# Rows of 34 chunks turned on VectorE and moved by SP transfers, in an attention and mixture-of-experts kernel

## The chip, the cores and the metric

The kernel runs on one core of one Trainium2 chip. The metric is the device time of one execution in microseconds (us); times are medians of several runs. The engines are PE (TensorE, matrix products; PEld is its loading of weights), DVE (VectorE), ACT (ScalarE), POOL (GpSimd) and SP (SyncE, which here only issues DMA transfers). SBUF is the working memory with 128 partitions, PSUM the memory into which PE writes.

## The reference

Attention over channels gives x, 20224 rows of 256 numbers; a gate gives each row to one of eight experts, 2528 rows to each, and each expert applies two matrices.

```python
qn = q / (np.linalg.norm(q, axis=1, keepdims=True) + 1e-06)
kn = k / (np.linalg.norm(k, axis=1, keepdims=True) + 1e-06)
s = kn.transpose(0, 2, 1) @ qn / tau
a = softmax(s)                       # over the last axis
x = (v @ a).reshape(B * S, D)        # 20224 x 256

logits = x @ w_gate
# pairs (row, expert) in descending order of logit: a row goes to the first
# expert that still has room, at most N // E = 2528 rows to each
for e in range(E):
    mask = assigned == e
    h = np.maximum(x[mask] @ w1[e], 0.0)
    out[mask] = h @ w2[e]
```

## The kernel before

The kernel has three parts. First the scores, the softmax and the gates' logits are worked out. Then x is made and stored in DRAM (x_d). Then the eight experts follow (p = 0 to 7), and beside them the routing (which rows belong to the next experts) goes on in `route` and `compact`, mostly on DVE, with short products on PE.

An expert's 2528 rows are 20 tiles of 128 (the last has 96), and the tiles are cut into chunks: (2, 4, 4, 4, 4, 2) for expert 0 and (4, 4, 4, 4, 4) for the others, 41 chunks in all. A chunk (p, c) goes through these steps:

- `load_x` (L999) queues one indirect DMA per tile on POOL, which gathers the rows into xg (three buffers); `gather` (L1008) issues the next one of the queue at fixed places of the order.
- `turn` (L1020) brings 128 of the 256 columns (kb 0 or 1) of all rows of a chunk to partitions: PE transposes tile by tile into pt in PSUM, ACT writes xH (the rounded high part), and DVE writes xL (what is left). After kb 1 it calls `load_x` for the chunk three further on, whose xg this one frees.
- `layer1` (L1048) has eight blocks (fb 0 to 7) of six products each into ph (three buffers); ACT makes hH = relu(ph), and DVE hL, the remainder.
- `layer2` (L1083) has 24 products per tile into py (two buffers); ACT copies py to y (six buffers), and POOL scatters y to out by an indirect DMA.

The chunks are taken in a staggered manner: layer 1 of chunk c, then layer 2 of chunk c - 1, with the two turns of chunk c + 1 before tiles 0 and 3 of that layer 2. The head of the next expert (p + 1, 0) is turned in the last layer 2 of expert p, between its tiles, and (p + 1, 1) in the blocks 2 and 7 of its own expert's first layer 1.

Every engine works through its instructions in the order in which the program emits them. That order is written out by hand: `Order` (L841) keeps estimated clocks for PE (`o.pe`) and DVE (`o.dve`). `o.post(ready, cost, fn, unit)` puts a DVE step into a first-in first-out list, from which it is emitted when the estimated clock of DVE reaches it; `o.flush(unit)` emits all up to a unit; steps of the routing fill the gaps between. `want(key, fn)` runs fn as soon as a result of the routing stands in the order.

SP has loads to issue only up to the attention part; while the experts run it issues none.

Of the kernel before, what the change touches and what calls it, by code (L numbers as in the profile page):

```python
# [8 lines left out]
F32 = mybir.dt.float32  # L9
# [6 lines left out]
OP = mybir.AluOpType  # L16
# [58 lines left out]
EARLY_PRIO = 4  # L75
COMPACT_PRIO = 2
SLACK = 450
DEPTH = 3


@with_exitstack
def attention_moe(ctx: ExitStack, tc: tile.TileContext, q, k, vt, tau, wg, w1t, w2t, tabs, out):
# [865 lines left out]
    def cols_of(p, c):  # L948
        a = sum(cuts[p][:c])
        return range(a, a + cuts[p][c])  # L950

    def n_in(col):
        return 128 if col < NCOL - 1 else LASTC
# [45 lines left out]
    def load_x(p, c):  # L999
        idx = routed[p]["src"]  # L1000
        xg = ffx.tile([128, 4, C], F32, name="xg", bufs=3)
        for i, col in enumerate(cols_of(p, c)):
            queue.append(lambda i=i, col=col, n=n_in(col): P.indirect_dma_start(  # L1003
                out=xg[:n, i, :], out_offset=None, in_=x_d,
                in_offset=bass.IndirectOffsetOnAxis(ap=idx[:n, col:col + 1], axis=0)))
        xgs[p, c] = xg

    def gather(behind=None):  # L1008
# [7 lines left out]
    phs = []  # L1016
    turned = [0]
    lows = {}

    def turn(p, c, kb):  # L1020
        xg = xgs[p, c]
        nt = n_of(p, c)
        if kb == 0:
            xH = ffx.tile([128, 2, 512], F32R, name="xH")
            xL = ffx.tile([128, 2, 512], F32R, name="xL")
            xts[p, c] = (xH, xL)
        xH, xL = xts[p, c]
        o.flush(turned[0])
        pt = ps_t.tile([128, 512], F32, name="pt")
        for i, col in enumerate(cols_of(p, c)):  # L1030
            n = n_in(col)
            PE.transpose(pt[:, i * 128:i * 128 + n].bitcast(F32R), xg[:n, i, kb * 128:(kb + 1) * 128].bitcast(F32R),  # L1032
                         identr[:n, :n])
        S.activation(xH[:, kb, 0:nt], pt[:, 0:nt], AF.Copy)  # L1034

        def low():
            V.tensor_tensor(xL[:, kb, 0:nt], pt[:, 0:nt], xH[:, kb, 0:nt].bitcast(F32), op=OP.subtract)  # L1037
        o.pe += 220
        o.hook()
        unit[0] += 1  # L1040
        turned[0] = unit[0]
        o.post(o.pe + TURN_LAT, 605, low, unit[0])
        ahead = chunks.index((p, c)) + 3
        if kb == 1 and ahead < len(chunks):
            p_, c_ = chunks[ahead]
            want(("idx", p_), lambda: load_x(p_, c_))

    def layer1(p, c, inserts):  # L1048
        o.flush(turned[0])
# [33 lines left out]
    def layer2(p, c, h, inserts):  # L1083
        hH, hL = h
        o.flush(lows[p, c])
        wH, wL = wt[p, 1]
        o.until(("out", p))
        idx = routed[p]["idx"]
        for i, col in enumerate(cols_of(p, c)):
            for fn in inserts.get(i, ()):  # L1090
                fn()
            n = n_in(col)
            tk = slice(i * 128, i * 128 + n)
            py = ps_2.tile([128, 512], F32, name="py")
            j = 0
            for fb in range(8):
                d = slice(fb * C, (fb + 1) * C)
                for l, w in ((hH, wH), (hH, wL), (hL, wH)):
                    PE.matmul(py[:n, 0:C], lhsT=l[:, fb, tk], rhs=w[:, d], start=(j == 0), stop=(j == 23))  # L1099
                    j += 1  # L1100
                    if j % 2 == 0:
                        o.tick(2 * 109)
            y = ffx.tile([128, C], F32, name="y", bufs=6)
            S.activation(y[:n], py[:n, 0:C], AF.Copy)  # L1104
            P.memset(spacer[:, 0:1], 0.0)  # L1105
            sd = P.indirect_dma_start(out=out, out_offset=bass.IndirectOffsetOnAxis(ap=idx[:n, col:col + 1], axis=0),  # L1106
                                      in_=y[:n], in_offset=None)
            for s_ in scat:
                tc.declare_no_dep(sd.ins, s_.ins, reason="each token is written once")
            scat.append(sd)  # L1110
            settle()
            gather()

    with tc.manual_schedule():
        o.dve = FIRST_LAT
        plan()
        cut_w = [None]

        def first_w():
            load_w(0)  # L1120
            cut_w[0] = [o.pe + LOAD_LAT] + list(SPLIT)

        want(("ei", 0), first_w)
        for i, (b, c) in enumerate(TODO):
            xs = vp.tile([128, T, GW], F32, name="xs", bufs=2)
            for t in range(0, T, 2):
                x_tiles(b, c, t, xs, C, o.tick)
                settle()
                if cut_w[0] and o.pe > cut_w[0][0] and len(cut_w[0]) > 1:
                    split_piece(0, *cut_w[0].pop(1))  # L1130
                if i + 1 == len(TODO) and t > 0:
                    store_x(b, c, xs, {2: 0, 4: 4, 6: 6}[t], t + 2)
            if i + 1 < len(TODO):
                store_x(b, c, xs)
        o.until(("ei", 0))
        settle()
        o.until(("idx", 0))
        actx.close()
        cctx.close()
        ffx = ctx.enter_context(tc.tile_pool(name="ffx", bufs=2))  # L1140
        ffx.tile([128, PAD_X], F32, name="pad_x", bufs=1)
        ps_1 = ctx.enter_context(tc.tile_pool(name="ps_1", bufs=3, space=PSUM))
        ps_2 = ctx.enter_context(tc.tile_pool(name="ps_2", bufs=2, space=PSUM))
        ps_t = ctx.enter_context(tc.tile_pool(name="ps_t", bufs=1, space=PSUM))
        o.margin = MARGIN
        for c in range(2):
            load_x(0, c)
            while queue:
                gather()
        load_x(0, 2)  # L1150
        for i, q_, eng in cut_w[0][1:]:
            split_piece(0, i, q_, eng)
        idle = ps_1.tile([128, 512], F32, name="ph")
        for i in range(START_TICKS):
            o.tick(200)
            PE.matmul(idle, lhsT=wt[0, 0][0][:, 0:128], rhs=wt[0, 0][0][:, 512:1024], start=(i == 0),
                      stop=(i == START_TICKS - 1))
        turn(0, 0, 0)
        turn(0, 0, 1)
        for p in range(E):  # L1160
            last = p == E - 1
            def turn_at(c, kb):
                return lambda: turn(p, c, kb)

            turns = [] if last else [0, 1]

            def next_turn(force=False):
                if not turns:
                    return
                if force:  # L1170
                    o.until(("idx", p + 1))
                    settle()
                    while queue:
                        gather()
                    while o.pe < routed[p + 1]["time"] + GATHER_LAT:
                        o.tick(100)
                if done.get(("idx", p + 1)) and o.pe >= routed[p + 1]["time"] + GATHER_LAT:
                    turn(p + 1, 0, turns.pop(0))

            if not last:  # L1180
                want(("ei", p + 1), lambda p=p: load_w(p + 1))
            nchunk = len(cuts[p])
            h = {}
            pieces = {} if p == 0 else {at: [lambda q_=q_: split_piece(p, 1, q_, None)] for q_, at in enumerate((1, 3, 4, 6))}
            h[0] = layer1(p, 0, {**pieces} if p == 0 else {2: [turn_at(1, 0)], 7: [turn_at(1, 1)], **pieces})
            for c in range(1, nchunk):
                if p == 0 and c == 1:
                    turn(p, 1, 0)
                    turn(p, 1, 1)
                    layer2(p, 0, h[0], {})  # L1190
                    h[1] = layer1(p, 1, {4: [turn_at(2, 0)], 7: [turn_at(2, 1)]})
                    continue
                h[c] = layer1(p, c, {})
                ins = {}
                if c + 1 < nchunk:
                    for at, kb in ((0, 0), (3, 1)):
                        ins.setdefault(min(at, cuts[p][c - 1] - 1), []).append(turn_at(c + 1, kb))
                elif not last:
                    def w1(p=p):
                        o.until(("ei", p + 1))  # L1200
                        settle()
                        g = split_w(p + 1, 0, V)
                        for _ in g:
                            o.dve += 600
                    ins = {min(1, cuts[p][c - 1] - 1): [w1]}
                layer2(p, c - 1, h[c - 1], ins)
            layer2(p, nchunk - 1, h[nchunk - 1], {i: [next_turn] for i in range(1, 4)})
            while turns:
                next_turn(True)

# [62 lines left out]
```

## Time and profile before

| | us |
|---|---|
| median of three runs | 1333.44 (1333.43 to 1334.2) |
| profiled execution | 1331.89 |
| its span, first to last instruction | 1330.1 |
| transposes of gathered rows on PE | 320, median 231 ns each, from 346 to 1290 us of the span |
| DMA engines, mean busy share while experts run | 0.18 to 0.20 |

The profile counts an engine as busy while an instruction runs on it; products on PE are pipelined, so two may overlap, and the pitch from one to the next says more than the duration of one. Rows of a timeline give start, duration, engine, line, operation, what is written and read, its form, and in brackets the idle time in front of it and what ended that.

### The profile page before, as it was taken

The page shows a single profiled execution, that of the slowest core. Times are in us where ns is not written, and L with a number is a line of the kernel's source. Part 1 is how long each engine was busy: PE and PEld are TensorE (multiplying, and loading weights), DVE is VectorE, ACT ScalarE, POOL GpSimd, SP SyncE. Part 2 cuts the span into 40 slices and gives each one's busy share as a digit, 9 for nine tenths or more (in the row PEclk, how much of TensorE's full clock was granted, in tenths as well). Part 3 has the DMA queues.
Part 4 walks back from the last instruction along what each step waited for, and adds up shares of the span by engine and source line. Part 5 has one row for each costly group of instructions (what it writes and reads, how often), then busy time and mean ns, then how long its engine had stood idle before and what let it go on. Part 6 is the DMA issues. An engine that isn't in the chain of part 4 may idle for free.

```text
span 1330.1 us, 23080 instructions
## 1 busy us (share of the span) xinstructions
PE 1301.9 (98%) x9162; PEld 1157.0 (87%) x9162; DVE 761.9 (57%) x1912; ACT 528.3 (40%) x1189; POOL 386.9 (29%) x642
## 2 busy tenths in 40 slices
PE   7989999999899999999999999999999999999998
PEld 6877877888788888998999898988998998999998
DVE  6765395768478568658757757673443224333321
ACT  5554452235234234425324524345543234334331
POOL 0000010000352443254333333343344334434222
PEclk9999999999999999999999999999999999999999
DMA  8999884235312112023111211131122113111000
GB/s 287 381 360 355 273 273 176 96 127 191 100 55 92 52 48 99 29 64 107 40 41 49 102 41 45 41 105 45 45 74 83 42 47 109 48 45 51 28 29 32
DMA packets 53707, 143.14 MB, mean 108 GB/s; under 512 B 7776, under 2 KB 28640, under 8 KB 48992
## 3 DMA queue, kind: packets, MB, share of 16 engines
q1 hardware_dynamic: 14544, 62.40, 13.4%
q0 software_dynamic: 17664, 58.22, 13.3%
q10 hardware_dynamic: 21392, 21.06, 4.6%
q8 instruction: 72, 1.18, 0.4%
q14 instruction: 35, 0.29, 0.1%
HBM read 99.97 MB, written 41.68 MB: 106 GB/s over the span
## 4 chain that ended last, share of the span: by engine, by line
PE 55%; issue 5%; POOL 2%; DVE 1%; ACT 0%; POOLq 0%
PE ph L1067 26%; PE py L1099 25%; PE pc L508 2%; PE pt L1032 1%; POOL out_dram L1106 1%; PE pi L717 1%; PE pc L521 0%; POOL spacer L1105 0%; DVE m L464 0%; DVE f L489 0%; DVE xL L1037 0%; POOLq L1268 0%; ACT hH L1070 0%; DVE eq L486 0%; DVE L L683 0%
## 5 line engine op out<-in xcount | busy, mean ns | idle before, releaser
L1099 PE MATMUL py<-ua,hH 128*128 128x256 f32 (+1 forms) x2560 | 469.4, 283 | 0.0
L1067 PE MATMUL ph<-xH,ua 128*128 128x512 f32 (+3 forms) x1312 | 412.5, 388 | 3.3 <-issue 1.9
L1099 PEld LDWEIGHTS py<-ua,hH 128*128 128x128 f32 (+1 forms) x2560 | 391.7, 187 | 0.4
L1099 PE MATMUL py<-ua,hL 128*128 128x256 f32 (+1 forms) x1280 | 360.4, 282 | 0.0
L1075 DVE SCALAR_TENSOR_TENSOR hL<-ph,hH 128x512 fp32r<-128x512 f32 (+3 forms) x328 | 219.3, 670 | 171.6 <-ACT hH L1070 140.4
L1067 PEld LDWEIGHTS ph<-xH,ua 128*128 128x128 f32 x1312 | 243.3, 188 | 48.7 <-DVE hL L1075 3.0
L1070 ACT ACTIVATE hH<-ph 128x512 fp32r<-128x512 f32 (+3 forms) x328 | 190.9, 583 | 232.2 <-PE ph L1067 208.9
L1106 POOL DMA_INDIRECT out_dram<-y,idx x160 | 159.7, 998 | 398.7 <-ACT y L1104 364.9
L1067 PE MATMUL ph<-xL,ua 128*128 128x512 f32 (+3 forms) x656 | 253.9, 387 | 0.3 <-DVE xL L1037 0.2
L1099 PEld LDWEIGHTS py<-ua,hL 128*128 128x128 f32 (+1 forms) x1280 | 239.5, 187 | 0.0
L1104 ACT ACTIVATE y<-py 128x256 f32<-128x256 f32 (+1 forms) x160 | 61.4, 384 | 341.2 <-PE py L1099 290.9
L1003 POOL DMA_INDIRECT xg<-x_d,src x160 | 161.0, 1006 | 97.7 <-issue 48.4
L250 PE MATMUL s<-ua 128*128 128x256 f32 (+1 forms) x640 | 146.6, 390 | 10.5 <-DMA ua<-in_q_dram 10.5
L250 PEld LDWEIGHTS s<-ua 128*128 128x128 f32 (+1 forms) x640 | 124.3, 196 | 31.2 <-issue 13.8
L1067 PEld LDWEIGHTS ph<-xL,ua 128*128 128x128 f32 x656 | 123.4, 188 | 21.4 <-DVE xL L1037 0.5
L1037 DVE TENSOR_TENSOR xL<-pt,xH 128x512 fp32r<-128x512 f32 (+3 forms) x82 | 54.6, 666 | 120.8 <-ACT xH L1034 120.5
L208 PE MATMUL px<-a,vr 128*128 128x256 f32 (+1 forms) x448 | 104.6, 388 | 2.3 <-ACT xs L212 2.3
L258 ACT ACTIVATE sq<-ua 128x1024 f32<-128x1024 f32 (+1 forms) x72 | 75.8, 1056 | 54.2 <-DMA ua<-in_k_dram 17.6
L208 PEld LDWEIGHTS px<-a,vr 128*128 128x128 f32 x448 | 83.5, 191 | 14.3 <-ACT xs L212 2.7
L212 ACT ACTIVATE xs<-px 128x512 f32<-128x512 f32 (+1 forms) x96 | 49.9, 527 | 91.1 <-PE px L208 88.6
L774 ACT ACTIVATE junk<-pi,rhalf 128x160 bf16<-128x160 f32 x140 | 54.1, 392 | 24.0 <-PE pi L717 22.0
L511 DVE TENSOR_TENSOR Dm<-pc,dmask 128x64 f32<-128x64 f32 (+3 forms) x63 | 12.8, 202 | 83.0 <-PE pc L508 59.1
(276 smaller groups left out, 1128.2 us busy)
## 6 DMA issues: line engine op xcount, KB each, us to landing
x_d<-xs ACTq DMA_DIRECT2D x19, 1024.0 KB, 4.6
ua<-in_k_dram SPq DMA_DIRECT2D x31, 512.0 KB, 6.2
ua<-in_q_dram SPq DMA_DIRECT2D x31, 512.0 KB, 7.3
vr<-in_vt_dram SPq DMA_DIRECT2D x14, 1024.0 KB, 11.1
ua<-in_vt_dram SPq DMA_DIRECT2D x4, 1024.0 KB, 4.8
ua<-in_k_dram SPq DMA_DIRECT2D x8, 480.0 KB, 5.4
ua<-in_q_dram SPq DMA_DIRECT2D x8, 480.0 KB, 7.1
xg<-x_d,src POOLq DMA_INDIRECT x160
```

Source lines behind the costliest of these rows:

```text
L208: mm = PE.matmul(px[:, i * C:i * C + width], lhsT=vs[b, c][:, kb, t + i, :], rhs=a_f[b][:, kb, 0:width], start=(kb == 0), stop=(kb == 1))
L250: newest[0] = PE.matmul(sb[:, ib * C:(ib + 1) * C], lhsT=kt[:np_, t, ib * 128:(ib + 1) * 128], rhs=qt[:np_, t, :], start=(first and t == 0 ...
L258: S.activation(sq[:np_], t_[:np_], AF.Square)
L774: S.activation(junk, pi[:, i * W:i * W + COLS], AF.Sign, bias=rhalf[:, g0 + i:g0 + i + 1], scale=-1.0, accum_out=sgn[:, g0 + i:g0 + i + 1])
L1003: queue.append(lambda i=i, col=col, n=n_in(col): P.indirect_dma_start(out=xg[:n, i, :], out_offset=None, in_=x_d, in_offset=bass.IndirectO ...
L1037: V.tensor_tensor(xL[:, kb, 0:nt], pt[:, 0:nt], xH[:, kb, 0:nt].bitcast(F32), op=OP.subtract)
L1067: PE.matmul(ph[:, 0:nt], lhsT=l[:, w], rhs=x_[:, kb, 0:nt], start=(i == 0), stop=(i == 5))
L1070: S.activation(hH[:, fb, 0:nt], ph[:, 0:nt], AF.Relu)
L1075: V.scalar_tensor_tensor(hL[:, fb, 0:nt], ph[:, 0:nt], 0.0, hH[:, fb, 0:nt].bitcast(F32), op0=OP.max, op1=OP.subtract)
L1099: PE.matmul(py[:n, 0:C], lhsT=l[:, fb, tk], rhs=w[:, d], start=(j == 0), stop=(j == 23))
L1104: S.activation(y[:n], py[:n, 0:C], AF.Copy)
L1106: sd = P.indirect_dma_start(out=out, out_offset=bass.IndirectOffsetOnAxis(ap=idx[:n, col:col + 1], axis=0), in_=y[:n], in_offset=None)
```

## The change

Three chunks, (0, 0), (0, 1) and (0, 2), go on by PE (`BY_PE`). For others, `stage` may take the place of the transposes. It has two halves, each one instruction on DVE that turns the 32 x 32 blocks of 128 columns of all tiles from xg into xs. After the second half, SP issues 16 transfers of 32 partitions each, SBUF to SBUF, from xs to xT, which put each block row on the partitions where a full transpose has it. `split_x` then makes xH and xL from xT as `turn` did from pt.

`stage` refuses the first half where the gathers of the chunk are not yet taken as landed when the order is written (6000 ns after the last issue by the estimated clock of PE). A refused half is tried again at the next of the listed places as long as enough places are left for both halves. A chunk that was not staged goes through `turn` as before (`ready_x` chooses).

The places are the blocks 0, 2 and 4 of layer 1 of the chunk before (for the head of an expert: of the last layer 1 of the expert before), and for (p + 1, 1) the tiles 2 and 3 of the last layer 2 of expert p. The splits stand before tiles 1 and 2, or 2 and 3, of the layer 2 that follows. The second half also calls `load_x` for the chunk three further on. Where a chunk's last tile has 96 rows, POOL first zeroes the other 32 partitions of it in xg. y has four buffers in place of six; xs and xT have one each. The change's name says that 34 chunks are staged.

```diff
+SPLIT_X_LAT = 900
+STAGE_AT = (0, 2, 4)
+LAND_LAT = 6000
+BY_PE = {(0, 0), (0, 1), (0, 2)}
...
         xg = ffx.tile([128, 4, C], F32, name="xg", bufs=3)
+        if cuts[p][c] * 128 > n_of(p, c) and (p, c) not in BY_PE:
+            P.memset(xg[96:128, cuts[p][c] - 1, :], 0.0)
+
+        def fetch(i, col, n):
+            P.indirect_dma_start(out=xg[:n, i, :], out_offset=None, in_=x_d,
+                                 in_offset=bass.IndirectOffsetOnAxis(ap=idx[:n, col:col + 1], axis=0))
+            landed[p, c] = o.pe + LAND_LAT
         for i, col in enumerate(cols_of(p, c)):
...
+            queue.append(lambda i=i, col=col, n=n_in(col): fetch(i, col, n))
...
+        if kb == 1:
+            load_ahead(p, c)
+
+    def load_ahead(p, c):
         ahead = chunks.index((p, c)) + 3
-        if kb == 1 and ahead < len(chunks):
+        if ahead < len(chunks):
             p_, c_ = chunks[ahead]
             want(("idx", p_), lambda: load_x(p_, c_))
+
+    def by_pe(p, c):
+        return (p, c) not in staged
+
+    def stage(p, c, half):
+        if (p, c) in BY_PE or half == 0 and landed.get((p, c), 1e12) > o.pe or half == 1 and (p, c) not in staged:
+            return False
+        if half == 0:
+            staged[p, c] = (ffx.tile([128, 1024], F32, name="xs", bufs=1), ffx.tile([128, 1024], F32, name="xT", bufs=1))
+        xs, xT = staged[p, c]
+        k = cuts[p][c]
+        xg = xgs[p, c]
+
+        def flip():
+            V.transpose(xs[:, 0:k * 256].rearrange("p (q b i e) -> p b i q e", q=4, b=2, i=k)[:, half],
+                        xg[:, 0:k, half * 128:(half + 1) * 128])
+            if half == 1:
+                w = k * 64
+                for t in range(4):
+                    for q in range(4):
+                        nc.sync.dma_start(xT[q * 32:q * 32 + 32, t * w:(t + 1) * w],
+                                          xs[t * 32:t * 32 + 32, q * w:(q + 1) * w])
+                load_ahead(p, c)
+        unit[0] += 1
+        o.post(o.pe, 190 * k, flip, unit[0])
+        return True
+
+    def stager(p, c, ats):
+        halves = [0, 1]
+        late = []
+
+        def go(at):
+            if halves and len(ats) - ats.index(at) >= len(halves) and stage(p, c, halves[0]):
+                halves.pop(0)
+                late.append(at)
+        return {at: [lambda at=at: go(at)] for at in ats}, late
+
+    def split_x(p, c, kb):
+        xT = staged[p, c][1]
...
+        rows = xT[:, 0:k * 256].rearrange("p (t b i e) -> p b i t e", t=4, b=2, i=k)[:, kb]
+        S.activation(xH[:, kb, 0:k * 128].rearrange("p (i t e) -> p i t e", i=k, t=4), rows, AF.Copy)
+
+        def low():
+            V.tensor_tensor(xL[:, kb, 0:k * 128].rearrange("p (i t e) -> p i t e", i=k, t=4), rows,
+                            xH[:, kb, 0:k * 128].rearrange("p (i t e) -> p i t e", i=k, t=4).bitcast(F32), op=OP.subtract)
+        unit[0] += 1
+        turned[0] = unit[0]
+        o.post(o.pe + SPLIT_X_LAT, 700, low, unit[0])
+
+    def ready_x(p, c, kb):
+        (turn if by_pe(p, c) else split_x)(p, c, kb)
...
-            y = ffx.tile([128, C], F32, name="y", bufs=6)
+            y = ffx.tile([128, C], F32, name="y", bufs=4)
...
+            h[0] = layer1(p, 0, pieces if p == 0 else inserts(
+                {2 if by_pe(p, 1) else 5: [turn_at(1, 0)], 7: [turn_at(1, 1)]}, pieces))
...
-                h[c] = layer1(p, c, {})
+                at, late = stager(p, c + 1, STAGE_AT) if c + 1 < nchunk else stager(p + 1, 0, STAGE_AT) if not last else ({}, 0)
+                h[c] = layer1(p, c, at)
                 ins = {}
                 if c + 1 < nchunk:
-                    for at, kb in ((0, 0), (3, 1)):
+                    for at, kb in ((0, 0), (3, 1)) if not late else ((1, 0), (2, 1)) if max(late) < 4 else ((2, 0), (3, 1)):
                         ins.setdefault(min(at, cuts[p][c - 1] - 1), []).append(turn_at(c + 1, kb))
...
-            layer2(p, nchunk - 1, h[nchunk - 1], {i: [next_turn] for i in range(1, 4)})
+            ahead = None if last else stager(p + 1, 1, (2, 3))[0]
+            layer2(p, nchunk - 1, h[nchunk - 1], {} if last else {
+                1: [next_turn], 2: [next_turn] + ahead[2], 3: [next_turn] + ahead[3]})
```

More of the change, by code (lines that the diff above doesn't have):

```diff
@@ L1001, in load_x @@
         xg = ffx.tile([128, 4, C], F32, name="xg", bufs=3)
+        if cuts[p][c] * 128 > n_of(p, c) and (p, c) not in BY_PE:
[4 more added lines that the diff above has]
+            landed[p, c] = o.pe + LAND_LAT
         for i, col in enumerate(cols_of(p, c)):
-            queue.append(lambda i=i, col=col, n=n_in(col): P.indirect_dma_start(
-                out=xg[:n, i, :], out_offset=None, in_=x_d,
-                in_offset=bass.IndirectOffsetOnAxis(ap=idx[:n, col:col + 1], axis=0)))
+            queue.append(lambda i=i, col=col, n=n_in(col): fetch(i, col, n))
         xgs[p, c] = xg
@@ L1018, in attention_moe @@
     lows = {}
+    landed = {}
+    staged = {}
     def turn(p, c, kb):
@@ new lines, in stager @@
+    def stager(p, c, ats):
[8 more added lines that the diff above has]
+        xT = staged[p, c][1]
+        k = cuts[p][c]
+        if kb == 0:
+            xH = ffx.tile([128, 2, 512], F32R, name="xH")
+            xL = ffx.tile([128, 2, 512], F32R, name="xL")
+            xts[p, c] = (xH, xL)
+        xH, xL = xts[p, c]
+        o.flush(turned[0])
+        rows = xT[:, 0:k * 256].rearrange("p (t b i e) -> p b i t e", t=4, b=2, i=k)[:, kb]
[6 more added lines that the diff above has]
+        o.post(o.pe + SPLIT_X_LAT, 700, low, unit[0])
@@ L1162, in turn_at @@
             def turn_at(c, kb):
-                return lambda: turn(p, c, kb)
+                return lambda: ready_x(p, c, kb)
             turns = [] if last else [0, 1]
@@ L1177, in next_turn @@
                 if done.get(("idx", p + 1)) and o.pe >= routed[p + 1]["time"] + GATHER_LAT:
-                    turn(p + 1, 0, turns.pop(0))
+                    ready_x(p + 1, 0, turns.pop(0))
             if not last:
@@ L1184, in attention_moe, with inserts @@
             pieces = {} if p == 0 else {at: [lambda q_=q_: split_piece(p, 1, q_, None)] for q_, at in enumerate((1, 3, 4, 6))}
-            h[0] = layer1(p, 0, {**pieces} if p == 0 else {2: [turn_at(1, 0)], 7: [turn_at(1, 1)], **pieces})
+            def inserts(*dicts):
+                d = {}
+                for e in dicts:
+                    for at, fns in e.items():
+                        d.setdefault(at, []).extend(fns)
+                return d
+            h[0] = layer1(p, 0, pieces if p == 0 else inserts(
+                {2 if by_pe(p, 1) else 5: [turn_at(1, 0)], 7: [turn_at(1, 1)]}, pieces))
             for c in range(1, nchunk):
@@ L1192, in attention_moe @@
                     continue
-                h[c] = layer1(p, c, {})
+                at, late = stager(p, c + 1, STAGE_AT) if c + 1 < nchunk else stager(p + 1, 0, STAGE_AT) if not last else ({}, 0)
+                h[c] = layer1(p, c, at)
                 ins = {}
                 if c + 1 < nchunk:
-                    for at, kb in ((0, 0), (3, 1)):
+                    for at, kb in ((0, 0), (3, 1)) if not late else ((1, 0), (2, 1)) if max(late) < 4 else ((2, 0), (3, 1)):
                         ins.setdefault(min(at, cuts[p][c - 1] - 1), []).append(turn_at(c + 1, kb))
+                if c + 1 < nchunk:
+                    pass
                 elif not last:
```

## The prediction

> **What bounds the kernel now.** I read the page's busy times first, then the busy times by stretch over the expert layers, and then the waits of PE there.
>
> ```profile
> span 1330.1 us, 23080 instructions
> ## 1 busy us (share of the span) xinstructions
> PE 1301.9 (98%) x9162; PEld 1157.0 (87%) x9162; DVE 761.9 (57%) x1912; ACT 528.3 (40%) x1189; POOL 386.9 (29%) x642
> ```
>
> The next two rows are stretches: start and end, length, then busy time and instructions of PE, PEld, DVE, ACT and POOL, the granted clock, the DMA share and GB/s. The first is expert 2, with the routing of later experts beside it; the second is expert 5, without.
>
> ```profile
> 610.00:735.00 125.00, 125.00 (x1027) 112.93 (x1027) 91.61 (x259) 54.22 (x157) 48.38 (x78) 1.00 0.18 59
> 984.00:1098.00 114.00, 114.00 (x760) 104.67 (x759) 38.64 (x58) 40.38 (x78) 45.03 (x78) 1.00 0.20 64
> ```
>
> What PE waited for from 484 to 1211 us (experts 1 to 6; total, times, longest):
>
> ```profile
> PE ph L1067 <- DVE hL L1075: 0.5, 1, 0.5
> PE pi L717 <- ACT ext L777: 0.4, 1, 0.4
> PE pc L521 <- DVE Ex L517: 0.3, 1, 0.3
> PE ph L1067 <- DVE xL L1037: 0.2, 1, 0.2
> ```
>
> The reader is to see that PE waits 1.4 us in 727 us. It is the bound there at full clock, DVE has room (73% busy in expert 2, 34% in expert 5), and the DMA engines are a fifth busy. What leaves PE's stream leaves the time, unless something new makes PE wait.
>
> **What is removed: 68 turns on PE.** A full chunk takes two turns (kb 0 and 1) of four transposes each. I price a turn by what it does to the cadence of ACT, which reads out each product right as PE ends it; these are rows of ACT's timeline, in expert 7.
>
> ```profile
> 1257.71 0.60 ACT L1070 ACTIVATE hH<-ph 128x512 fp32r<-128x512 f32 x1 [0.77 <-PE ph L1067]
> 1258.20 0.60 ACT L1034 ACTIVATE xH<-pt 128x512 fp32r<-128x512 f32 x1
> 1260.90 0.38 ACT L1104 ACTIVATE y<-py 128x256 f32<-128x256 f32 x1 [2.10 <-PE py L1099]
> ...
> 1266.60 0.38 ACT L1104 ACTIVATE y<-py 128x256 f32<-128x256 f32 x1 [2.50 <-PE py L1099]
> 1266.88 0.59 ACT L1034 ACTIVATE xH<-pt 128x512 fp32r<-128x512 f32 x1
> 1269.79 0.38 ACT L1104 ACTIVATE y<-py 128x256 f32<-128x256 f32 x1 [2.31 <-issue]
> ...
> 1303.11 0.57 ACT L1070 ACTIVATE hH<-ph 128x480 fp32r<-128x480 f32 x1 [0.73 <-PE ph L1067]
> 1305.99 0.38 ACT L1104 ACTIVATE y<-py 128x256 f32<-128x256 f32 x1 [2.31 <-PE py L1099]
> 1308.81 0.38 ACT L1104 ACTIVATE y<-py 128x256 f32<-128x256 f32 x1 [2.44 <-PE py L1099]
> ```
>
> From the last hH to the first y is 3.19 us with a turn between (1257.71 to 1260.90) and 2.88 without (1303.11 to 1305.99): 0.31. From y to y is 3.19 with one (1266.60 to 1269.79) and 2.82 without (1305.99 to 1308.81): 0.37. So a chunk's two turns cost PE 0.68 us. The change's name gives 34 chunks: 34 x 0.68 = **23.1 us off PE** (21.1 if all were 0.31, 25.2 if all 0.37). That number fits the code: of 41 chunks, (0,0), (0,1) and (0,2) are fixed to PE and (0,3) to (7,4), 38, may be staged. (1,1) cannot, as its slots are tiles 2 and 3 of a last chunk (0,5) that has two tiles; three more would not have landed when the order is written, most likely heads of early experts.
>
> **What is added on DVE: 68 flips.** The nearest row is the same operation on the same shape, read from PSUM (count: min/median/max ns):
>
> ```profile
> L357 DVE STREAM_TRANSPOSE lt<-px x8: 706/716/718, 176.4 to 235.6; 128x512 f32<-128x512 f32 x8
> ```
>
> The new split reads SBUF in place of PSUM. The rows for xL as it is, and for the same subtraction with two SBUF operands in the weights' split:
>
> ```profile
> L1037 DVE TENSOR_TENSOR xL<-pt,xH 128x512 fp32r<-128x512 f32 x64 | 43.9, 685 | 89.8 <-ACT xH L1034 89.5
> ...
> L985 DVE TENSOR_TENSOR ua<-ub,ua 128x512 fp32r<-128x512 f32 x56 | 36.6, 685 | 13.5 <-ACT ua L982 13.5
> ```
>
> Both 685 ns, so the split stays as it is. The flip from SBUF with scattered blocks has no row: bounds are half the row (0.36 us) and twice it (1.4 us); I take 0.72, as operation and size are the same. That is 68 x 0.72 = 49 us of DVE in some 850 us, 1.4 us a chunk. It is off the path while it fits. A flip is emitted in layer 1, in front of an hL, and waits there for its gathered rows; behind it stand hL and the routing's steps, and PE waits for hL, since ph has three buffers. The room, from ACT's and DVE's rows of one block:
>
> ```profile
> 1021.82 0.60 ACT L1070 ACTIVATE hH<-ph 128x512 fp32r<-128x512 f32 x1 [0.72 <-PE ph L1067]
> 1023.18 0.60 ACT L1070 ACTIVATE hH<-ph 128x512 fp32r<-128x512 f32 x1 [0.76 <-PE ph L1067]
> ```
>
> ```profile
> 1022.45 0.69 DVE L1075 SCALAR_TENSOR_TENSOR hL<-ph,hH 128x512 fp32r<-128x512 f32 x1 [0.62 <-ACT hH L1070]
> ```
>
> The block's hL ends at 1023.14. Its buffer is wanted when two further blocks of 1.36 us (1021.82 to 1023.18) are done, at about 1021.8 + 2.7 = 1024.5. So 1.3 us of room against 0.72: hidden without routing, tight where the routing fills DVE's gaps. At 1.4 a flip would outrun it by 0.1 us, 7 us over 68.
>
> **What is added on SP: 16 transfers of 32 KB a chunk, 544 in all.** SP issues nothing else then. Its rows at the kernel's start, when nothing held it, its quickest and its slowest single issue of such loads, and the page's smallest SP loads with the time to landing:
>
> ```profile
> 2.13 0.43 SPq L245 DMA_DIRECT2D ua<-in_q_dram  x1
> 2.60 0.43 SPq L245 DMA_DIRECT2D ua<-in_k_dram  x1
> ```
>
> ```profile
> 146.55 0.33 SPq L245 DMA_DIRECT2D ua<-in_k_dram  x1
> 146.93 1.23 SPq L245 DMA_DIRECT2D ua<-in_q_dram  x1
> ```
>
> ```profile
> ua<-in_k_dram SPq DMA_DIRECT2D x1, 128.0 KB, 2.4
> ua<-in_q_dram SPq DMA_DIRECT2D x1, 128.0 KB, 3.3
> ```
>
> Pitch 0.47 us (bounds 0.37 and 1.27, from 0.33 and 1.23 with the same 0.04 us gap). Sixteen take 7.5 us, and the last lands some 2.4 us later: 10 us from the second flip to a whole xT. The dates, from layer 1's start: slots 0 and 2, the second flip ends at 2 x 1.36 + 0.72 + up to 0.7 behind an hL = 4.2; xT stands at 14.1. Layer 1 lasts 10.9, a tile of layer 2 is 2.82, so the split at tile 1 is met by ACT at 13.7. It waits some 0.4 us. Queued behind it on ACT is the y of tile 1, which PE needs only when tile 3 begins (two py buffers), at 10.9 + 3 x 2.82 = 19.4; ACT needs 0.6 + 0.4 us for xH and y, so xT may come as late as 18.4. With slots 2 and 4 the same sum gives 16.8 for xT and 16.6 for its split at tile 2. Room 4 us: hidden. For the second chunk of an expert the flip ends about 9.5 us into the last layer 2 (11.3 long), xT stands at 19.5, and its split in block 5 of the next layer 1 comes at 11.3 + 6.8 = 18.1; ACT reaches it after a hH, at 18.8. That is up to 0.7 us of waiting, with hH behind it, inside the 1.3 us of room. The transfers move some 17.7 MB in 1 KB rows, and ACT's queue shows what such packets take (packets, MB, share of 16 engines):
>
> ```profile
> q10 hardware_dynamic: 21392, 21.06, 4.6%
> ```
>
> About 3.9% of the engines, then, with a fifth in use: no bound.
>
> Here the Trainium skill speaks against the change: "DMA: Bandwidth & Descriptors", section "Rules for kernel authors", says to join small transfers into large ones, as below 64 KB one mostly pays overhead, and its section on the anatomy of a DMA gives about 2.0 us fixed for each. If that were paid one after another it would be 16 x 2.0 = 32 us a chunk, and by the room worked out above PE would wait 17.8 us a chunk and the kernel take some 1.9 ms, an estimate from the page; it is the extreme of the slow rival below. The two SP rows, 0.47 us apart while a load takes over 2 us to land, speak for overlap.
>
> **The small edits.** load_x moves from the turn to the second flip, earlier than before; the memset of the padding rows (eight, on POOL) waits there for that flip, with gathers and scatters behind it, and POOL is 40% busy. y goes from six buffers to four:
>
> ```profile
> L1106 POOL DMA_INDIRECT out_dram<-y,idx x160: 908/961/1722, 361.5 to 1326.3; - x160
> ```
>
> The last scatter starts at 1326.3 and the span ends at 1330.1, so a y is free at most 3.8 + 0.6 us after ACT began it, against 4 x 2.82 = 11.3. If POOL stood 7 us, PE would wait for the rest. The routing's date: expert 1's rows are known at 440.4, and PE turns them at 480.0.
>
> ```profile
> L811 DVE COPY_PREDICATED src<-early,w__3920 x1: 173/173/173, 440.4 to 440.4; 128x20 int32<-128x20 int32 x1
> ```
>
> ```profile
> 479.99 0.46 PE L1032 MATMUL pt<-identr,xg 128*128 128x128 f32 x4
> ```
>
> Those 39 us cover the 3 x 1.4 us that flips add to DVE in expert 0.
>
> **The sum.** Profiled execution 1331.9 us (span 1330.1 and 1.8 around it) - 23.1 for the turns + 2 for scattered waits of hL and xH (chosen between 0 and the 11 below, nearer to today's 1.4) = 1310.8. The median of the runs is 1.5 higher than the profiled one: **1312 us**.
>
> **The rivals.** First, flips crowd DVE under the routing. For: 73% busy in expert 2, and DVE works in order. Against: 1.3 us of room, hL waits of 0.5 us now. Some 16 staged chunks, 32 flips, in experts 1 to 4, each half a flip too late: 11.5 us, **1324 us**. A long wait would cost more by the clock; PE's one long pause, and the stretch after it (clock 0.60):
>
> ```profile
> 462.84 0.37 PE L1067 MATMUL ph<-xH,ua 128*128 128x224 f32 x1 [1.85 <-issue]
> ```
>
> ```profile
> 463.00:467.20 4.20, 4.20 (x24) 4.20 (x25) 2.42 (x9) 0.85 (x3) 2.57 (x4) 0.60 0.23 66
> ```
>
> 4.2 us at 0.60 lose 1.7 us. The Trainium skill ("TensorE: Matmul & The Clock Gate", on HAM oscillation) warns of idle gaps over about 3.4 us; here the half-rate stretch follows a pause of 1.85 us.
>
> Second, the slow one: **SP's pitch**. The slack is 4 us over 16 issues, so at a pitch p ACT makes PE wait from 4.2 + 16 p + 2.4 = 18.4 on, p = 0.74, and the gain of 0.68 a chunk is gone at p = 0.78. For: single issues of 1.23 us, and 16 in a row are seen nowhere. Against: the first issues at 0.47. At 0.95 it costs 34 x 16 x 0.17 = 92 us: **1426 us**. Third, the change does not do all it says, with the heads of experts left to PE: seven chunks fewer give back 4.8 us, **1317 us**. Fourth, waits eat just the gain: 0.68 us a chunk, **1333 us**.
>
> **Chances.** Forecast 0.68 (own range 1308 to 1320, where the third rival lies too, 0.04), DVE 0.14 (1320 to 1329), no gain 0.05, slow 0.09. What a measurement can tell from no change is about 0.2%, 2.7 us. Faster 0.86, same 0.05, slower 0.09. The range, 1306 (all turns at 0.37, no waits) to 1326, leaves out some 0.18.
>
> **What would show it.** After: 52 transposes on PE, not 320 (268 of them go, as (0,5) has two tiles); y to y at 2.82 in every tile; expert 5 in about 110.6 us, not 114; flips of 0.72 us; SP issues 0.47 apart in trains of 7.5 us; waits of PE below 5 us. Wrong it would be with PE waiting for ACT's xH behind transfers (SP), for hL behind flips (DVE), or for y behind scatters.

## The result

The changed kernel takes 1350.09 us (median of four runs, 1344.19 to 1355.43) against 1333.43 for the kernel before (1330.41 to 1334.2): 1.0128 times as long, interval 1.0082 to 1.0175. On another chip (run e10 below) the ratio was 1.0171 (1.0132 to 1.021). The forecast was 1312 us, range 1306 to 1326, with a chance of 0.09 for slower. It was wrong in sign.

The page of the changed kernel, the lines that answer to those shown of before:

```profile
span 1346.6 us, 23608 instructions
## 1 busy us (share of the span) xinstructions
PE 1290.9 (96%) x8894; PEld 1142.0 (85%) x8894; DVE 803.4 (60%) x1980; ACT 530.4 (39%) x1189; POOL 393.7 (29%) x643
```

268 instructions have left PE, and PE is busy for 11.0 us less. But it is idle for 55.7 us of the span, where it was idle for 28.2: 27.5 more. 27.5 - 11.0 is the 16.5 us by which the span has grown. The two profiled executions took 1348.49 and 1331.89 us, 16.6 apart.

What PE waits for, from 340 us on (total, times, longest), the longest of the changed kernel's list:

```profile
PE pi L721 <- ACT ext L781: 13.8, 6, 3.3
PE ph L1140 <- DVE hL L1148: 4.7, 2, 3.0
PE pc L525 <- DVE Ex L521: 3.2, 7, 0.7
```

The first was 0.4 us before. pi is the routing's product, and ext is ACT's reading of it; so PE waits for ACT. ACT in turn waits for the new transfers. Its and SP's waits on xT (us in total, times, longest):

```profile
ACT xH L1109 <- DMA xT<-xs: 72.7, 30, 4.4
```

```profile
SPq L1082 <- DMA xT<-xs: 38.9, 48, 3.7
```

Each way from the transfers to PE can be followed once in the timelines. First the head of expert 6, where the second chunk's transfers are late. SP's row, then the end of the chain of waits there (start, duration, what), then ACT and PE:

```profile
1112.14 10.02 SPq L1082 DMA_DIRECT2D xT<-xs  x16
```

```profile
1120.93 0.59 SPq L1082
1121.52 0.04 issue
1121.57 4.82 DMA xT<-xs
```

```profile
1121.57 0.60 ACT L1143 ACTIVATE hH<-ph 128x512 fp32r<-128x512 f32 x1 [0.24 <-PE ph L1140]
1126.56 0.63 ACT L1109 ACTIVATE xH<-xT 128x512 fp32r<-128x512 f32 x1 [4.40 <-DMA xT<-xs]
1127.10 0.58 ACT L1143 ACTIVATE hH<-ph 128x512 fp32r<-128x512 f32 x1
```

```profile
1128.57 0.50 PE L1140 MATMUL ph<-xH,ua 128*128 128x512 f32 x1 [2.96 <-DVE hL L1148]
```

SP issues for 10.0 us, and ACT can go on only at 1126.56, 14.4 us after the first issue. The next hH stands behind that xH on ACT, hL behind hH, and PE finds ph's three buffers full. Then the clock falls as well. Two stretches after PE's pause (the last number but two is the granted clock, 0.60 in the first; the second begins 0.7 us later, and there it is 0.50):

```profile
1128.50:1132.00 3.50, 3.19 (x8) 2.12 (x9) 3.03 (x6) 1.51 (x4) 2.29 (x5) 0.60 0.25 44
1129.20:1132.50 3.30, 3.07 (x8) 2.04 (x7) 2.53 (x5) 1.09 (x3) 2.79 (x5) 0.50 0.40 107
```

Second, a place where the routing runs beside, ACT and PE in expert 1:

```profile
540.51 0.63 ACT L1109 ACTIVATE xH<-xT 128x512 fp32r<-128x512 f32 x1 [3.81 <-DMA xT<-xs]
541.05 0.16 ACT L781 ACTIVATE ext<-pi 128x6 f32<-128x6 f32 x1
```

```profile
541.26 0.37 PE L721 MATMUL pi<-E__97,G 128*128 128x162 bf16 x3 [3.09 <-ACT ext L781]
```

Here ext, 0.2 us of work, stands behind the xH that waits 3.8 us for its rows, and PE's next pi, which needs the only buffer that ext reads, waits 3.1 us.

### The profile page after: what moved, and what is told of

Same layout as the page of the kernel before. It is cut to its first block, busy times and chain, and to the rows that moved or that the text cites. A ratio compares the mean times of both kernels' runs of the same rounds, so it can differ in the third digit from the quotient of the medians.

```text
span 1346.6 us, 23608 instructions
## 1 busy us (share of the span) xinstructions
PE 1290.9 (96%) x8894; PEld 1142.0 (85%) x8894; DVE 803.4 (60%) x1980; ACT 530.4 (39%) x1189; POOL 393.7 (29%) x643
## 3 DMA queue, kind: packets, MB, share of 16 engines
q0 software_dynamic: 17664, 58.22, 13.3%
## 4 chain that ended last, share of the span: by engine, by line
PE 60%; SPq 11%; DMA 9%; issue 9%; DVE 6%; ACT 3%; POOL 2%; ACTq 0%; POOLq 0%; DVEq 0%
PE py L1172 22%; PE ph L1140 18%; SPq L1082 11%; PE px L212 8%; PE s L254 8%; DMA xT<-xs 4%; DMA ua<-in_q_dram 2%; DMA x_d<-xs 2%; PE pc L512 2%; POOL out_dram L1179 1%; PE px L358 1%; DVE hL L1148 1%; DVE xL L1112 1%; ACT xH L1109 1%; ACT hH L1143 1%
## 5 line engine op out<-in xcount | busy, mean ns | idle before, releaser
L1172 PEld LDWEIGHTS py<-ua,hH 128*128 128x128 f32 (+1 forms) x2560 | 397.7, 189 | 5.1 <-ACT y L1177 1.6
L1112 DVE TENSOR_TENSOR xL<-xT,xH 128x512 fp32r<-128x512 f32 (+1 forms) x68 | 46.4, 682 | 145.1 <-ACT xH L1109 132.2
L262 ACT ACTIVATE sq<-ua 128x1024 f32<-128x1024 f32 (+1 forms) x72 | 75.8, 1057 | 56.2 <-DMA ua<-in_k_dram 24.0
L1109 ACT ACTIVATE xH<-xT 128x512 fp32r<-128x512 f32 (+1 forms) x68 | 42.3, 622 | 72.7 <-DMA xT<-xs 72.7
L1020 POOL COPY spacer<-hH 1x1 f32<-1x1 f32 x109 | 22.4, 205 | 139.5 <-ACT hH L1143 131.1
```

The costliest lines, as they stand in the source:

```text
L262: S.activation(sq[:np_], t_[:np_], AF.Square)
L1112: V.tensor_tensor(xL[:, kb, 0:k * 128].rearrange("p (i t e) -> p i t e", i=k, t=4), rows, xH[:, kb, 0:k * 128].rearrange("p (i t e) -> p i ...
```

## The experiments

Theory 1: the train of 16 issues and its landing is late, ACT stands in front of xT with all that is queued behind, and PE waits for ACT and then runs at half clock. Theory 2: the 68 flips crowd DVE. Theory 3: the bytes on the DMA engines, or the buffers of y. The runs fell on three chips: e1 to e4 on the first, e5 to e8 on the second, e9 to e12 on the third. The kernel before takes 1334.2, 1323.1 and 1322.8 us on them; so ratios to the kernel before on the same chip are what to compare. e1, e2 and e5 leave the rows on their partitions and so compute another output; they only price the parts.

| run | us | before, same chip | ratio, interval |
|---|---|---|---|
| e1, no transfers | 1311.48 | 1334.24 | 0.9824 (0.9805 to 0.9843) |
| e2, one transfer | 1311.39 | 1334.24 | 0.9824 (0.9806 to 0.9842) |
| e3, second chunks by PE | 1331.82 | 1334.24 | 0.9983 (0.9968 to 0.9997) |
| e4, staging beside PE's turns | 1346.69 | 1334.24 | 1.0091 (1.0073 to 1.011) |
| e5, eight transfers | 1301.99 | 1323.09 | 0.9837 (0.982 to 0.9853) |
| e6, five through DRAM | 1304.93 | 1323.09 | 0.9869 (0.9853 to 0.9886) |
| e7, started earlier | 1305.39 | 1323.09 | 0.9864 (0.9847 to 0.988) |
| e8, splits later | 1309.48 | 1323.09 | 0.9893 (0.9876 to 0.9909) |
| e10, the change again | 1343.15 | 1322.83 | 1.0171 (1.0132 to 1.021) |
| e11, DRAM and later splits | 1301.56 | 1322.83 | 0.9839 (0.9823 to 0.9856) |
| e9, flips beside PE's turns | 1323.67 | 1322.83 | 1.001 (1.0 to 1.002) |
| e12, e4 again | 1324.12 | 1322.83 | 1.0008 (0.9997 to 1.0018) |

### Without the transfers, and with one

e1 takes the 16 transfers out; e2 puts one transfer of the same bytes in their place.

```diff
-                for t in range(4):
-                    for q in range(4):
-                        nc.sync.dma_start(xT[q * 32:q * 32 + 32, t * w:(t + 1) * w],
-                                          xs[t * 32:t * 32 + 32, q * w:(q + 1) * w])
+                nc.sync.dma_start(xT[:, 0:4 * w], xs[:, 0:4 * w])      # e2 only; in e1 xT is xs
```

> The changed kernel without the 16 transfers per chunk: the split reads xs, so rows stay on their partitions and the output is another one; flips, splits, places and y buffers are unchanged. Theory 1 (the train of transfers is late, ACT waits for it with everything behind, PE waits for ACT or hL and then runs at half clock for 3.4 us): 1310 to 1316 us, ACT's 73 us of waits for xT gone, at most two half-clock stretches. Theory 2 (68 flips on DVE crowd hL and the routing): 1335 us or more, waits of PE for hL and Ex as in the changed kernel. Theory 3 (four y buffers, memsets on POOL): 1335 us or more, with waits of ACT y for scatters.

> The changed kernel with one SP transfer of 128 partitions and the same 512 KB per chunk, xs to xT on the same partitions, in place of 16 of 32 KB (so the rows are not moved across partitions, and the output is another one). Theory 1 with the number of issues as the cause (16 x 0.635 us): 1310 to 1318 us, waits of ACT for xT under 10 us. If it is the bytes on the DMA engines (beside weights and gathers) that land late: 1325 us or more, with waits for xT of 30 us or more. Theory 2 (flips): 1335 or more.

Both give 1311.4 us, 22.8 below the kernel before, with all 68 flips and with y in four buffers. So theory 2 and theory 3 fall: neither the flips, nor the buffers, nor (in e2) the 17.6 MB cost anything that can be seen. All of the loss, 1.0128 - 0.9824 or some 40 us, lies in moving the same bytes by 16 issues. These also differ from e2's in that they move rows of 1 KB, not 4 KB, and across partitions; e8 below, which keeps them as they are, tells whether that matters. PE's waits of e2 from 340 us on:

```profile
PE py L1169 <- issue: 2.5, 5, 1.1
PE pt L1043 <- DVE xL L1048: 2.2, 2, 1.3
PE pc L525 <- DVE Ex L521: 1.8, 4, 0.7
PE pt L1043 <- DMA xg<-x_d,src: 0.9, 2, 0.6
PE ph L1226 <- ACT xs L216: 0.7, 1, 0.7
PE ph L1137 <- DVE xL L1048: 0.5, 2, 0.3
PE pi L721 <- ACT ext L781: 0.3, 1, 0.3
```

The wait of pi for ext is back at 0.3 us, and ACT waits for xT nowhere.

### Second chunks left to PE

```diff
-BY_PE = {(0, 0), (0, 1), (0, 2)}
+BY_PE = {(0, 0), (0, 1), (0, 2)} | {(p, 1) for p in range(1, E)}
```

> The changed kernel with the second chunks of experts 1 to 7 left to PE, whose xT comes 4 us late in the first layer 1 of experts 5 and 6 (PE waits 1.8 and 3.0 us, each with a half-clock stretch). Theory 1: six chunks give back 6 x 0.68 = 4 us, and the stalls at the heads of experts go, 5 us of waits and two half-clock stretches of 1.7 us with what hangs on them: 1340 to 1346 us. Theory 2: six of 34 chunks fewer flips, about a sixth of the loss of 40 us less and 4 us back: also 1343 to 1350, but with waits for hL still there.

The result, 19 us below the changed kernel by the ratios of the two (0.9983 and 1.0128 of 1334), is much better than I expected. Six second chunks go back to PE and one more head of an expert is staged, so it is five chunks fewer (464 issues in place of 544), and they take away nearly half of the loss. A second chunk has the least room by the prediction, 1.3 us against 4. Also ACT's waits for xT go from 72.7 to 48.2 us, and SP's for its own earlier transfers from 38.9 to 13.3.

### The staging beside PE's turns, and the flips alone beside them

In e4 and e12 `ready_x` always calls `turn`, at the old places, and `turn` alone calls `load_x` for the chunk three further on, as in the kernel before. 35 chunks are staged beside it, with 560 issues, and nobody reads xT. In e9 the transfers are left out too.

```diff
...
-        (turn if by_pe(p, c) else split_x)(p, c, kb)
+        turn(p, c, kb)
...
```

> The changed kernel with all chunks turned by PE as before, at the old places, and the staging (flips, 16 transfers) done beside it, its result unused; y has four buffers. It prices flips, transfers and buffers without any wait for xT. Theory 1: 1333 to 1338 us, as before. Theory 2 or 3: 1345 us or more, since PE has its 23 us of turns back.

> All chunks turned by PE at the old places, with the 68 flips beside it and no transfers. The same with transfers was 1.009 of before, where theory 1 expected 1.000 to 1.003. If the flips on DVE make that difference (beside PE's turns): 1.007 to 1.011. If the trains of 16 transfers do, without any wait for xT: 0.998 to 1.003.

> All chunks turned by PE, flips and 16 transfers beside it, once more, for a comparison on one chip with the flips alone: 1.007 to 1.011 of before, if the chip makes no difference.

On the third chip e9 and e12 take what the kernel before takes, to 0.1%: there trains that nobody waits for cost nothing that can be seen, and the flips do not either. On the first chip the same kernel, e4, was 0.9% longer, as long as theory 2 or 3 had it, and e12's expectation, that the chip makes no difference, failed. In e4's trace PE waits 6.6 us for Ex and 3.1 us for ext, in e12's 0.7 us for ext. The longest of the waits for Ex, 3.0 us, stands behind DVE and ACT, which both stood until 870.4 us. The product pc that DVE reads there was done 4.2 us before; the profile names nothing that held them (remote and issue name no instruction of the program):

```profile
865.47 0.67 PE L512 MATMUL pc<-oh,ge 128*128 128x16 bf16 x20
870.37 0.17 DVE L515 TENSOR_TENSOR Dm<-pc,dmask 128x16 f32<-128x16 f32 x1 [6.77 <-remote]
870.47 0.60 ACT L1142 ACTIVATE hH<-ph 128x512 fp32r<-128x512 f32 x1 [4.22 <-issue]
871.04 0.28 PE L525 MATMUL pc<-Ex,ones_q 128*128 128x32 f32 x1 [3.00 <-DVE Ex L521]
```

What makes the first chip's execution differ was not found, and it stays open. e1 and e2 show that the flips cost nothing there without PE's turns; the flips alone beside PE's turns were not run on that chip. So an effect of the trains of their own, of up to 12 of the 40 us, is not excluded on the first chip. On the third chip e12, with the trains, takes what e9 takes without them, and the changed kernel (e10) is still 42 us behind e11.

### Eight transfers

```diff
+                for q in range(4):
+                    for t in range(2):
+                        nc.sync.dma_start(xT[q * 32:q * 32 + 32, t * 2 * w:(t + 1) * 2 * w],
+                                          xs[q * 32:q * 32 + 32, t * 2 * w:(t + 1) * 2 * w])
```

> The changed kernel with 8 SP transfers of 32 partitions and 64 KB per chunk, same bytes, xs to xT on the same partitions (rows are not moved across partitions, so the output is another one). Theory 1, the train of issues: 8 x 0.635 = 5.1 us instead of 10.2, xT stands some 5 us earlier, inside the 4 us of room that the one-transfer kernel does not even need: 1311 to 1318 us, waits of ACT for xT under 25 us. If each transfer's landing rather than the train were late: 1325 us or more.

0.9837: half as many issues, each of the same length, and the whole loss is gone. ACT waits for xT once, 2.1 us. So the cost does not grow in step with the number of issues. What fits is that it begins when the train outlasts the time that the order leaves for it; e7 and e8 test this.

### The same 16 transfers, started earlier or waited for later

e7 stages a chunk in tiles 2 and 3 of the layer 2 before, one layer 1 earlier, and leaves second chunks to PE. e8 only moves the splits.

```diff
# e7
...
-            ahead = None if last else stager(p + 1, 1, (2, 3))[0]
+            ahead = None if last else stager(p + 1, 2, (2, 3))[0]
...
+                    if c + 2 < nchunk:
+                        for at, fns in stager(p, c + 2, (2, 3))[0].items():
+                            ins.setdefault(at, []).extend(fns)
# e8
-  if not late else ((1, 0), (2, 1)) if max(late) < 4 else ((2, 0), (3, 1)):
+  if not late else ((2, 0), (3, 1)) if max(late) < 4 else ((3, 0), (3, 1)):
...
-                {2 if by_pe(p, 1) else 5: [turn_at(1, 0)], 7: [turn_at(1, 1)]}, pieces)
+                {2: [turn_at(1, 0)], 7: [turn_at(1, 1)]} if by_pe(p, 1) else {7: [turn_at(1, 0), turn_at(1, 1)]}, pieces)
```

> The 16 transfers kept, but flips and transfers of a chunk start one layer 2 earlier (tiles 2 and 3 of the layer 2 before), so that the train has the whole layer 1 for itself; second chunks of experts 1 to 7 go by PE, and the third ones are staged in the last layer 2 of the expert before. Some 29 chunks staged. Theory 1: the train is as long but nobody waits for it: 1334 - 29 x 0.68 = 1314, 1312 to 1322 us. If the issues themselves disturb (SP's semaphores, small packets in front of gathers, weights or instruction loads): 1325 us or more.

> The changed kernel with the splits one tile later (tiles 2 and 3, or both at 3, and both at block 7 for second chunks): 2.8 us more for the train before ACT meets its wait, with 34 chunks staged. Theory 1: much of the loss goes, 1318 to 1335 us, waits of ACT for xT from 73 to under 40 us. If the issues disturb by themselves: 1345 us or more.

This is the sharpest test, as the transfers are the same, 16 a chunk, and in e8 only the time between issue and use differs. e7 is at 0.9864 with 29 chunks staged: 18.0 us gained of 29 x 0.68 = 19.7. e8 is at 0.9893 with all 34, which is 1320 of 1334 and at the good end of what I expected; ACT's waits for xT fall to 7.1 us, though SP still waits for its own transfers 68 times, 50.7 us in all. What is left in e8 is PE waiting for xH and xL at the head of layer 1, 4.3 us, as the splits are now a little late.

### Five transfers through DRAM

```diff
+                xd = dram.tile([128, 1024], F32, name="xd", bufs=2)
+                nc.sync.dma_start(xd[:, 0:4 * w], xs[:, 0:4 * w])
+                blocks = xd[:, 0:4 * w].rearrange("(t e) (q w) -> q e t w", t=4, q=4)
+                for q in range(4):
+                    nc.sync.dma_start(xT[q * 32:q * 32 + 32, 0:4 * w].rearrange("e (t w) -> e t w", t=4), blocks[q])
```

> The changed kernel with the full transpose kept, but moved by five transfers per chunk through DRAM: one of 128 partitions from xs, then four of 32 partitions into xT with runs of 1 KB. The train is 0.5 us + about 3 us for the store to land + 4 x 0.64 + about 3 us = 9 us instead of 13 to 14. Theory 1: 1311 to 1320 us. A rival, that traffic from weights and gathers makes any transfer land late: 1325 us or more.

> The five transfers through DRAM (0.987 of before) with the splits one tile later, and at blocks 6 and 7 for second chunks. Theory 1: the few waits left with the train through DRAM (5.6 us of ACT for xT, one half-clock stretch) go: 0.983 to 0.987 of before. If the later splits make PE wait for xH or xL at the head of layer 1, as the later places with 16 transfers did (2.8 and 1.5 us): 0.988 to 0.992.

e6 does the whole rearrangement and is at 0.9869; e11, with the splits one tile later as in e8 (second chunks at blocks 6 and 7), is at 0.9839, 21.3 us below the kernel before. It is the fastest of the kernels that compute everything, and faster than both the kernel before and the changed one. PE's waits in e11 from 340 us on:

```profile
PE pt L1043 <- DVE xL L1048: 2.2, 2, 1.3
PE ph L1230 <- ACT xs L216: 0.7, 1, 0.7
PE pt L1043 <- DMA xg<-x_d,src: 0.6, 1, 0.6
PE ph L1141 <- DVE xL L1113: 0.6, 3, 0.2
PE ph L1141 <- DVE xL L1048: 0.2, 1, 0.2
```

Its page and that of e10, the changed kernel on the same chip, give the size of the two parts of the loss:

```profile
span 1299.4 us, 23056 instructions
## 1 busy us (share of the span) xinstructions
PE 1275.7 (98%) x8894; PEld 1133.7 (87%) x8894; DVE 806.4 (62%) x1980; ACT 530.5 (41%) x1189; POOL 390.5 (30%) x642
```

```profile
PE 1287.5 (96%) x8894; PEld 1140.4 (85%) x8894; DVE 804.8 (60%) x1980; ACT 531.7 (40%) x1189; POOL 394.7 (29%) x643
```

e10's expectation and its result:

> The changed kernel once more, beside the others on one chip: its ratio to the kernel before was 1.013. Theory 1 (late train): 1.009 to 1.017 of before again, with ACT's waits for xT at 50 us or more.

e10 is at 1.0171, just above the 1.017 at which its range ended, and ACT waits 75.1 us for xT. Its span is 1341.1 us. The same 8894 instructions of PE are busy 11.8 us longer, and PE is idle 53.6 us in place of 23.7, 29.9 more; together 41.7. The clock accounts for the busy part: its mean was 0.989 in e10 and 0.997 in e11, and 0.8% of 1341 us is 11 us.

## Why the prediction was wrong

**The turns: right.** 34 chunks, 268 transposes gone, 52 left. The price of 0.68 us a chunk, 23.1 us, is what e1 and e2 gained: 22.8 us against the kernel before. My sum for the change would have been right to 1.4 us had nobody waited for the transfers. (The lower end of the range, 1306, does not follow from what it is said to be: all turns at 0.37 and no waits give 1312 - 2.1 - 2 = 1308.)

**The flips and splits: right.** 702 ns in the median where I took 0.72 us, and splits of 692 ns where I took 685; e1 and e9 show that DVE hides them:

```profile
L1076 DVE STREAM_TRANSPOSE xs<-xg x68: 432/702/714, 382.5 to 1291.0; 128x512 f32<-128x512 f32 x66, 128x256 f32<-128x256 f32 x2
```

**The small edits: right.** ACT waited 0.5 us in all for a free y. The routing ends later (expert 7's rows are known at 1057 us, not 975) without PE waiting for them.

**The train of transfers: the step that failed.** The prediction put it as "Sixteen take 7.5 us, and the last lands some 2.4 us later: 10 us from the second flip to a whole xT." The runs show this for the issues, in the changed kernel and in e2:

```profile
L1082 SPq DMA_DIRECT2D xT<-xs x544: 507/589/1950, 386.4 to 1301.2; - x182
```

```profile
L1080 SPq DMA_DIRECT2D xT<-xs x34: 464/465/537, 387.9 to 1255.8; - x34
```

With the 0.04 us between two issues it is 0.63 us for each of 32 partitions, where I took 0.47 from loads of 128 partitions. So 16 take 10 us in place of 7.5. Then SP stood 48 times on an earlier transfer of its own, up to 3.7 us, which I had no term for; the issues of a train took 10.0 to 12.1 us. In the train shown above the last landed 4.8 us after its issue, where I took 2.4; that was while a weight matrix was being gathered, which may be why, but no run separates that. There it was 14.4 us from the first issue, the longest of all. In the changed kernel's trace ACT waited for 30 of the 34 trains, and with these its xH began 11.5 to 14.5 us after the second flip's end, 12.5 in the median, in place of 10.

**The room: the second step that failed.** For a chunk within an expert I wrote that ACT may come 4 us late, because PE next needs the y of tile 1 when tile 3 begins. 2.5 us more for the train would still have fitted into that. It holds where nothing else is queued on ACT. Expert 6 shows it:

```profile
1147.25 0.63 ACT L1109 ACTIVATE xH<-xT 128x512 fp32r<-128x512 f32 x1 [2.28 <-DMA xT<-xs]
1147.79 0.37 ACT L1177 ACTIVATE y<-py 128x256 f32<-128x256 f32 x1
1148.05 0.63 ACT L1109 ACTIVATE xH<-xT 128x512 fp32r<-128x512 f32 x1
```

2.3 us late, and PE ran through. But I listed y alone as queued behind the waiting xH. The routing's steps are queued there as well, and PE's pi stands on ext with a single buffer, and has no room at all: that made 13.8 us of PE's waits, where e2 has 0.3. For second chunks I worked out a room of 1.3 us and a wait of up to 0.7; in the train shown the wait was 4.4, by the 4.4 us that this train took longer than my 10.

**The rivals.** The slow one had the right mechanism: the transfers outlast their time, ACT stands, PE stands behind it. I gave it 0.09, because I made it depend on SP's pitch alone and on y alone, and so put its break-even at 0.78 us an issue. The pitch was 0.63, and the kernel was already 40 us behind what it would have been. The clock, which I priced at 1.7 us for one pause, added some 11 us. The rival of a crowded DVE fell with e1 and e9. That three heads of early experts would be left to PE was right. Of the Trainium skill's rule on joining small transfers ("DMA: Bandwidth & Descriptors", section "Rules for kernel authors") the direction holds here: one transfer of the same bytes cost nothing, sixteen cost 40 us. The fixed price of 2.0 us that the prediction took from the Trainium skill, same page, stands there in a section on transfers that GpSimd issues, while these are SP's. It did not add up in series, as the issues went out 0.63 us apart.

## What to carry to other kernels

A train of transfers that nobody waits for cost nothing on the third chip (e12 against e9), and e7 kept 18.0 of 19.7 us with it; one that is late costs as much as the most urgent thing queued behind its waiter on an engine that works in order, and the half clock after it. So work out the date of a train of transfers from issues of the same shape and with its own slots, list everything that is queued behind the wait, not only the stage's own steps, and leave a whole stage between issue and use, or use fewer transfers: e7, e8 and e11 turn a loss of 1.3 to 1.7% into a gain of 1.1 to 1.6% with the same idea.

## What the runs showed of the hardware

An SP issue of a transfer between SBUF tiles took 0.589 us in the median with 32 partitions (32 KB, and also 64 KB in e5: 0.590) and 0.465 us with 128 partitions and 512 KB, so the larger one is the quicker to issue. In the changed kernel's trace the granted clock stood at 0.5 for 3.4 us seven times while the experts ran: six times after a pause of PE of 1.8 to 3.3 us, once after one of 1.3. After one of 2.1 us it did not, so the length of the pause alone does not decide it. With a mean of 0.989 in place of 0.997, PE was busy 11.8 us longer in one whole execution with the same instructions. And one kernel (e4 and e12) stood at 1.009 of before on one chip and at 1.001 on another, so a difference of under 1% that was measured on one chip need not hold on the next.
